# Value products always in split parts, a sixth head pair with float32 scores, and TensorE's products grouped by kind

## The chip, the cores and the metric

The kernel runs on one core of a Trainium2 chip. Its time is the device time of that core in microseconds (us); the median of three runs before the change is 1055.27 us (1054.64 to 1059.42). The core has a matrix engine (TensorE, PE in the rows, its weight loads PEld), a vector engine (VectorE, DVE), an engine for functions of one operand (ScalarE, ACT), a general one (GpSimd, POOL) and a queue that issues the DMAs (SyncE, SP). Each runs its own list of instructions in order and waits on semaphores for the others.

## The reference

Queries are averaged over pairs of rows, attention is taken in float32 for 4 batches of 8 heads (576 pooled queries, 1152 keys, 64 dimensions), and the result goes through two dense layers with a leaky ReLU between them.

```
q_pool = q.reshape(B, H, S // 2, 2, D).mean(axis=3)          # B 4, H 8, S 1152, D 64
scores = q_pool @ k.transpose(0, 1, 3, 2) / sqrt(D)
scores = scores - max(scores, axis=-1)
attn = exp(scores); attn = attn / (sum(attn, axis=-1) + 1e-9)
x = (attn @ v).transpose(0, 2, 1, 3).reshape(B * S // 2, H * D)   # 2304 x 512
h = x @ w_in                                                  # 512 x 2048
out = maximum(0.01 * h, h) @ w_out                            # 2048 x 512
```

## The kernel before

Results have to be as exact as float32. The kernel has two ways to a product. In the float32 way both operands stay float32. In the split way an operand is written as a first part, rounded to the shorter type fp32r, and a second part, the rest, and the products of the parts are summed in one bank of PSUM.

Attention is cut into 54 units, each one head with a group of its queries: a group of 256 rows (two tiles of 128) or one of 320 (tiles of 108, 106 and 106). For three batches the groups of 256 rows of all head pairs come first and those of 320 after. A segment is a head pair with one group (in the last batch with both); `PLAIN` is the number of segments, from the first one on, that work in float32. With `PLAIN = 5` these are units 0 to 7 (256 rows) and 8 and 9 (320 rows).

A unit runs through these steps. Queries are summed in pairs on GpSimd (`q_sum`, L370), transposed (`q_tr`, L378), and copied out of PSUM (`q_hi`, `q_lo`). Keys are transposed (`k_tr`, L328) and copied, whole for a float32 segment (`k_cp`) or in eight pieces of first and second parts (`k_hi`, `k_lo`, L343). `qk` makes the scores of a tile: in float32 two products of 512 columns and one of 128 (L428), in split parts six of 384 columns (L437 to L442). `vmax` takes the row maxima on VectorE (L453, and the last small one L457), `exp` the exponentials and their sums on ScalarE (L468). `tr` transposes the exponentials (L505); `e_hi` copies a transposed block to SBUF, in float32 on whichever of ScalarE and VectorE is free, in split parts as a cast on ScalarE, and `e_lo` then makes the second part on VectorE (L514). `pvm` multiplies by the values: in float32 one product a key tile (L525, two records each in the trace), in split parts two (L531) against a block that holds the first and second parts of the values side by side, 64 columns each. Those are made by `v_hi` (a cast on ScalarE or VectorE) and `v_lo` (L405, GpSimd). For a float32 segment `norm_plain` (L551, VectorE) multiplies by the reciprocal sums; for a split one `norm` first copies the lower half (ScalarE), adds it to the upper (L543, VectorE) and multiplies on GpSimd (L546).

Besides, 32 chunks of the weights are brought into shape and split (L579 to L604: ScalarE, VectorE twice, ScalarE, GpSimd, a cast, GpSimd), the first 16 for the first layer, which are stored in DRAM and read back, the others for the second. The two layers run over nine blocks of 256 rows: `l1` (L652) needs the block's rows of all heads, `l2` (L674 to L676) the split weights.

What stands where is decided by a planner written into the kernel, the class `Scheduler`. Each step has a rank (`prio`), costs on the engines that can do it, and the steps and buffers that it needs. The planner keeps a clock per engine, and of the steps that can start soonest takes the one of lowest rank. Ranks are counted in tiles of attention: `AHEAD` is how much earlier the preparation of a unit stands, `SOONER` the maxima and exponentials, `TR`, `SPLIT`, `PV` where transposes, splits and value products stand; `WIN` and `WOUT` place the weight chunks of the first and second layer (start and step), `WAHEAD` how many of them may be loaded ahead. `EARLY` is the unit from which the second score buffer is given to transposes and the layers. All that decides the order only; the waits come from what an instruction reads and writes.

Of the kernel before, what the change touches and what calls it, by code (L numbers as in the profile page):

```python
# [22 lines left out]
PLAIN = 5  # L23

KEEP = True
RT = 2.5
EARLY = 7
FIRST = 0
AHEAD = 4.0
# [3 lines left out]
WAHEAD = 3  # L33
WIN = (0.0, 1.0)
WOUT = (16.0, 0.6)
# [12 lines left out]
class Scheduler:  # L48
# [7 lines left out]
    def __init__(self, tags):  # L56
# [6 lines left out]
        self.done, self.log = set(), []  # L63

# [29 lines left out]
    def run(self):  # L94
# [4 lines left out]
        while left:  # L99
# [11 lines left out]
            s, e, at = min((x for x in can if x[2] <= now), key=lambda x: x[0].prio)  # L111
# [5 lines left out]
            left -= 1  # L117

    def start(self, s, e, at, pending):
# [11 lines left out]
        end = self.free[e] = at + s.eng[e]  # L131
# [25 lines left out]
def tile_pooled_attention_moe(  # L157
# [341 lines left out]

    def tr(u, x, e, i):  # L500
# [17 lines left out]
    def pvm(u, x, e, i=None):  # L518
# [197 lines left out]
    for u in range(NU):  # L716
# [8 lines left out]
        if u == us[0]:  # L725
# [68 lines left out]
        step(r_tr, u, prio=p0 + RT, eng=trs(*[64 for x in tiles_of(u)]), deps=[("rsum", u, 1)], takes=[("t", [("r_cp", u)])])  # L794
        step(r_cp, u, prio=p0 - 1, eng={"ACT": act(w, True)}, deps=[("r_tr", u)], takes=[("rb", [("norm_plain", u) if plain(u) else ("norm", u, 2)])])
        nx = len(kts(u))
        for x in range(nx):
            nk = len(kts(u)[x])
            step(tr, u, x, prio=p0 + TR, eng=trs(*[y[1] for y in tiles_of(u)] * nk),
                 deps=[("exp", u, t, x) for t in range(ntile) for x in range(2)], order=[("tr", u, x - 1)] if x else [("r_tr", u)] if RT < 0 else [], takes=[("t", [("e_hi" if plain(u) else "e_lo", u, x)])])  # L800
            step(e_hi, u, x, prio=p0 + SPLIT, eng={"ACT": act(w * nk, True), "DVE": dve(w * nk, psum=True)} if plain(u) else {"ACT": act(w * nk, True)}, deps=[("tr", u, x)], takes=[("et", [("pvm", u, x)])])
            if not plain(u):
# [96 lines left out]
```

## Time and profile before

| | |
|---|---|
| median of three runs | 1055.27 us |
| the profiled execution: its time, its span | 1055.03 us, 1053.2 us |
| mean granted TensorE clock | 0.988 |
| busy, TensorE | 998.6 us, 95% of the span |
| busy, VectorE / ScalarE / GpSimd | 701.8 / 642.0 / 382.8 us |
| chain that ended last: TensorE / VectorE / ScalarE | 81% / 10% / 3% |

A busy share over the whole span is an average over stages that have different bounds, so the rows further down cut it. In rows of TensorE the duration of an instruction is partly modelled; how long a group holds the engine is the time from its start to the start of the next.

### The profile page before, as it was taken

Reading aid. Unit: us, or ns where it says so; the run is one execution under the profiler, and the core shown is the slowest. Engines: PE = TensorE matmul, PEld = TensorE weight load, DVE = VectorE, ACT = ScalarE, POOL = GpSimd, SP = SyncE. Lnnn points to the kernel's source line nnn. Section 1 sums busy time; section 2 is a strip of 40 time slices with the busy share of each in tenths; the row PEclk is TensorE's granted clock in tenths of the full one; section 3 lists DMA queues with packets and bytes.
Section 4 is the critical chain, followed back from the end, with each engine's and each line's share of the span. In section 5 each row is a group of like instructions: output and inputs, shape, how many; then the busy total and the mean of one; then the engine's idle time right before and its main releaser. Section 6 shows DMA issues by size and latency. Waiting matters only on the chain.

```text
span 1053.2 us, 18894 instructions
## 1 busy us (share of the span) xinstructions
PE 998.6 (95%) x6676; PEld 870.8 (83%) x6676; DVE 701.8 (67%) x1479; ACT 642.0 (61%) x1558; POOL 382.8 (36%) x382
## 2 busy tenths in 40 slices
PE   6999788899999999999999999999999999999998
PEld 3555367789889988989899897989999998889896
DVE  4777889888888667777877676786877766411110
ACT  5767767776777665776767666776767666311110
POOL 3555666532434242223335233232342321232320
PEclk8999799999999999999999999999999999999999
DMA  8878673146376353635567253341533312477640
GB/s 266 288 237 261 231 243 128 51 167 228 111 263 225 100 185 107 233 97 173 174 209 245 77 177 101 123 163 38 182 99 98 110 56 86 147 239 250 213 148 30
DMA packets 86383, 172.68 MB, mean 164 GB/s; under 512 B 8976, under 2 KB 45328, under 8 KB 86288
## 3 DMA queue, kind: packets, MB, share of 16 engines
q1 hardware_dynamic: 86288, 171.47, 49.9%
q8 instruction: 52, 0.85, 0.3%
q14 instruction: 43, 0.35, 0.1%
HBM read 144.18 MB, written 27.26 MB: 163 GB/s over the span
## 4 chain that ended last, share of the span: by engine, by line
PE 81%; DVE 10%; ACT 3%; issue 3%; DMA 2%; POOL 1%; SPq 1%; DVEq 0%; ACTq 0%; POOLq 0%
PE banks L652 15%; PE banks L505 13%; PE banks L531 11%; PE banks L674 6%; PE banks L676 6%; PE banks L675 6%; PE banks L525 4%; PE banks L437 4%; PE banks L438 4%; DVE mx L453 3%; PE banks L428 3%; PE banks L441 2%; PE banks L442 2%; PE banks L328 2%; PE banks L486 2%
## 5 line engine op out<-in xcount | busy, mean ns | idle before, releaser
L453 DVE TENSOR_REDUCE mx<-banks 106x1 f32<-106x768 f32 (+4 forms) x320 | 235.3, 753 | 84.8 <-PE banks L438 45.7
L468 ACT ACTIVATE e<-banks,mx 106x768 f32<-106x768 f32 (+4 forms) x320 | 237.5, 744 | 54.2 <-DVE mx L457 47.4
L652 PE MATMUL banks<-xb,ws 128*128 128x256 f32 x1728 | 241.7, 285 | 11.3 <-ACT g L660 5.3
L652 PEld LDWEIGHTS banks<-xb,ws 128*128 128x128 f32 x1728 | 224.3, 190 | 19.7 <-ACT g L660 8.5
L200 ACT CAST et<-banks 128x320 fp32r<-128x320 f32 (+2 forms) x390 | 171.6, 466 | 101.2 <-PE banks L531 47.9
L514 DVE TENSOR_TENSOR et<-banks,et 128x320 fp32r<-128x320 f32 (+2 forms) x390 | 199.1, 528 | 50.5 <-ACT et L200 48.4
L505 PE MATMUL banks<-ident,e 128*128 128x128 f32 (+2 forms) x1440 | 204.6, 266 | 13.1 <-DVE mx L457 3.7
L531 PE MATMUL banks<-et,vv 128*128 128x320 f32 (+1 forms) x972 | 207.3, 320 | 3.2 <-DVE et L514 2.1
L505 PEld LDWEIGHTS banks<-ident,e 128*128 128x128 f32 (+2 forms) x1440 | 164.8, 141 | 50.8 <-DVE et L514 7.5
L531 PEld LDWEIGHTS banks<-et,vv 128*128 128x128 f32 x972 | 142.6, 189 | 6.9 <-DVE et L514 2.9
L370 POOL TENSOR_TENSOR qs<-qn 80x256 f32<-80x256 f32 (+1 forms) x128 | 75.6, 611 | 179.7 <-PE banks L378 100.3
L665 POOL TENSOR_TENSOR gg<-g,gg 128x512 fp32r<-128x512 f32 x60 | 77.8, 1297 | 155.9 <-DVE gg L200 112.7
L660 ACT ACTIVATE g<-banks 128x512 f32<-128x512 f32 x72 | 43.0, 597 | 99.9 <-PE banks L652 99.4
L405 POOL TENSOR_TENSOR vv<-vr,vv 128x576 fp32r<-128x576 f32 x46 | 66.3, 1442 | 100.0 <-DVE vv L200 65.9
L437 PE MATMUL banks<-kk,qq 128*106 128x384 f32 (+2 forms) x276 | 96.5, 350 | 2.0 <-ACT e L468 2.0
L674 PE MATMUL banks<-wo,gg 128*128 128x512 f32 x240 | 97.6, 407 | 0.0
L676 PE MATMUL banks<-wo,gg 128*128 128x512 f32 x240 | 94.4, 393 | 0.0
L675 PE MATMUL banks<-wo,gg 128*128 128x512 f32 x240 | 94.3, 393 | 0.0
L438 PE MATMUL banks<-kk,qq 128*106 128x384 f32 (+2 forms) x276 | 93.0, 337 | 0.0
L546 POOL TENSOR_TENSOR xo<-x,rb 64x320 f32<-64x320 f32 (+1 forms) x54 | 44.1, 816 | 71.6 <-DVE x L543 62.3
L468 ACT ACTIVATION_READ_ACCUMULATOR e<-banks,mx 128x1 f32 (+2 forms) x320 | 63.9, 200 | 0.0
L200 DVE CAST gg<-g 128x512 fp32r<-128x512 f32 x55 | 25.4, 462 | 47.8 <-ACT g L660 47.1
(70 smaller groups left out, 1364.1 us busy)
## 6 DMA issues: line engine op xcount, KB each, us to landing
ws<-wd SPq DMA_DIRECT2D x144, 512.0 KB, 4.5
vr<-in_v_dram SPq DMA_DIRECT2D x46, 288.0 KB, 3.4
kn<-in_k_dram SPq DMA_DIRECT2D x19, 576.0 KB, 4.1
kd<-kk SPq DMA_DIRECT2D x16, 576.0 KB, 5.2
kk<-kd SPq DMA_DIRECT2D x16, 576.0 KB, 4.1
raw<-in_moe_w_in_dram SPq DMA_DIRECT2D x16, 512.0 KB, 5.7
wd<-ws SPq DMA_DIRECT2D x16, 512.0 KB, 4.0
raw<-in_moe_w_out_dram SPq DMA_DIRECT2D x16, 512.0 KB, 6.3
```

The source lines that it names most:

```text
L200: ENG[e].copy(out=out, in_=in_) if e == "ACT" else ENG[e].tensor_copy(out=out, in_=in_)
L437: nc.tensor.matmul(p[:, c], lhsT=hi, rhs=key[:, c * CW:(c + 1) * CW], start=True, stop=False)
L438: nc.tensor.matmul(p[:, c], lhsT=lo, rhs=key[:, c * CW:(c + 1) * CW], start=False, stop=True)
L453: nc.vector.tensor_reduce(out=m[:, part:part + 1], in_=sps[u, j, part], axis=(AX.XY, AX.X)[part], op=ALU.max)
L468: nc.scalar.activation(out=d, in_=sps.pop((u, j, part)), func=AF.Exp, bias=mxs[u, j][:n, 2:3], accum_out=st[u][:n, c:c + 1])
L505: nc.tensor.transpose(p[:, a * w + o:a * w + o + n], ex[u, j][:n, t * 128:(t + 1) * 128], ident[:n, :n])
L514: nc.vector.tensor_tensor(out=et[u, x][:, 1, :w], in0=tps.pop((u, x))[:, :w], in1=f32(et[u, x])[:, 0, :w], op=ALU.subtract)
L531: nc.tensor.matmul(p, lhsT=vv[vis_of[u]][:, korder[vis_of[u] % 2][t], :], rhs=et[u, x][:, y, a * w:(a + 1) * w], start=(t == 0 and y == 0) ...
L652: nc.tensor.matmul(p, lhsT=wst[i, f][:, a, c, :], rhs=xx[i][:, x, c, :], start=(n == 0), stop=(n == 3 * KC - 1))
L674: nc.tensor.matmul(p, lhsT=gh, rhs=wo[f][:, 0], start=(f == hf * FH), stop=False)
L675: nc.tensor.matmul(p, lhsT=gh, rhs=wo[f][:, 1], start=False, stop=False)
L676: nc.tensor.matmul(p, lhsT=gl, rhs=wo[f][:, 0], start=False, stop=(f == hf * FH + FH - 1))
```

## The change

`PLAIN` becomes 6, so that the sixth segment (a head pair with its 320 rows: units 10 and 11, six tiles) also gets float32 scores. A second number, `PLAINV = 0`, decides about the values alone: no unit has float32 value products any more. So in units 0 to 9 every transposed block is cast on ScalarE and gets a second part on VectorE, the values go through `v_hi` and `v_lo`, and `norm` has its three steps. The planner marks the float32 score products as a kind of their own: a change of kind on TensorE costs `TURN` on its clock, and a step of the other kind stands `KIND` later in rank. Several numbers of ranks and costs move as well.

```
-PLAIN = 5
+PLAIN = 6
+PLAINV = 0
+TURN = 0.145
+KIND = 0.5
-EARLY = 7
+EARLY = 5
-AHEAD = 4.0
+AHEAD = 5.0
-WAHEAD = 3
+WAHEAD = 2
-WOUT = (16.0, 0.6)
+WOUT = (22.0, 0.8)
...
+        self.kinds, self.kind = set(), False
...
-            s, e, at = min((x for x in can if x[2] <= now), key=lambda x: x[0].prio)
+            s, e, at = min((x for x in can if x[2] <= now), key=self.urgency)
...
+    def urgency(self, x):
+        return x[0].prio + (KIND if x[1] == "PE" and (x[0].key in self.kinds) != self.kind else 0.0)
...
-        end = self.free[e] = at + s.eng[e]
+        end = at + s.eng[e]
+        if e == "PE" and (s.key in self.kinds) != self.kind:
+            self.kind = not self.kind
+            end += TURN
+        self.free[e] = end
...
+    def plain_v(hd):
+        return hd < 2 * PLAIN and hd % 4 < PLAINV
+
+    def plainv(u):
+        return plain_v(vis_of[u])
...
-        et[u, x] = new("et", i, F32 if plain(u) else None)
+        et[u, x] = new("et", i, F32 if plainv(u) else None)
...
-            if plain(u):
+            if plainv(u):
                 nc.tensor.matmul(
-                    p[0:64], lhsT=vv[vis_of[u]][:, (0, 2, 4, 6, 1, 3, 5, 7, 8)[t], :], rhs=et[u, x][:, 0, a * w:(a + 1) * w],
+                    p[0:64], lhsT=vv[vis_of[u]][:, key_tile(u, t), :], rhs=et[u, x][:, 0, a * w:(a + 1) * w],
...
-                eng = mm4(swidth(u)[part]) if plain(u) else mm(*[CW] * (2 if part else 4))
+                eng = {"PE": 0.3 if part else 1.045} if plain(u) else mm(*[CW] * (2 if part else 4))
...
+                if plain(u):
+                    sch.kinds.add(("qk", u, t, part))
...
-            if not plain(u):
+            if not plainv(u):
                 step(e_lo, u, x, prio=p0 + SPLIT, eng={"DVE": dve(w * nk, psum=True)}, deps=[("e_hi", u, x)])
...
-        if plain(u):
+        if plainv(u):
             step(norm_plain, u, prio=p0, eng={"DVE": dve(w, psum=True)}, deps=[("pvm", u, nx - 1), ("r_cp", u)], takes=[("xo", [("x_out", u)])])
```

What the planner makes of it is seen in the lists of instructions. First TensorE, late among the units of 256 rows, before (banks are PSUM; e are the exponentials, et their transposed blocks, vv the values, kk and qq keys and queries, kn keys as loaded, stat the reciprocals of the sums):

```order
L428 MATMUL banks<-kk,qq 128x128
L328 MATMUL banks<-ident,kn 128x128 x3
L525 MATMUL banks<-et,vv 64x256 x2
L328 MATMUL banks<-ident,kn 128x128 x3
L486 MATMUL banks<-ident,stat_67 64x128 x2
L525 MATMUL banks<-et,vv 64x256 x3
L378 MATMUL banks<-ident,qs 128x80 x4
L428 MATMUL banks<-kk,qq 128x512 x2
L505 MATMUL banks<-ident,e 128x128 x4
```

and TensorE at about the same place after:

```order
L527 MATMUL banks<-ident,e 128x128 x4
L447 MATMUL banks<-kk,qq 128x128
L527 MATMUL banks<-ident,e 128x128 x10
L553 MATMUL banks<-et,vv 128x256 x8
L447 MATMUL banks<-kk,qq 128x512 x2
L505 MATMUL banks<-ident,stat_66 64x128 x2
L553 MATMUL banks<-et,vv 128x256 x4
L447 MATMUL banks<-kk,qq 128x128
L347 MATMUL banks<-ident,kn 128x128 x3
```

Of the nine rows before, four are of the float32 kind (L428, L525) and change with transposes at nearly every row; after, only the three rows of scores (L447) are, and the value products (L553, now two a key tile and 128 columns of values) stand with the transposes. Over the whole list changes of kind fall from 126 to 88. Next VectorE among the same units, before (mx are maxima, raw and ws weights, et the transposed blocks; the number behind a name is the buffer's):

```order
L457 TENSOR_REDUCE mx_681<-mx_681 128x1
L453 TENSOR_REDUCE mx_711<-banks_63 128x1
L200 CAST ws_723<-raw_643 128x512
L588 SCALAR_TENSOR_TENSOR raw_699<-raw_522,raw_699 128x512
L200 COPY et_732<-banks_63 128x512
L200 COPY et_738<-banks_63 128x256
L453 TENSOR_REDUCE mx_711<-banks_63 128x1
L457 TENSOR_REDUCE mx_711<-mx_711 128x1
```

and VectorE there after:

```order
L476 TENSOR_REDUCE mx_561<-mx_561 128x1
L610 SCALAR_TENSOR_TENSOR raw_599<-raw_457,raw_599 128x512
L536 TENSOR_TENSOR et_607<-banks_63,et_607 128x512
L536 TENSOR_TENSOR et_615<-banks_63,et_615 128x512
L472 TENSOR_REDUCE mx_633<-banks_63 128x1
L213 CAST ws_643<-raw_599 128x512
L606 TENSOR_SCALAR raw_647<-raw_589 128x512
L610 SCALAR_TENSOR_TENSOR raw_647<-raw_496,raw_647 128x512
L536 TENSOR_TENSOR et_656<-banks_63,et_656 128x256
L472 TENSOR_REDUCE mx_633<-banks_63 128x1
L496 SCALAR_TENSOR_TENSOR stat1_66<-stat1_66 128x2
```

Some plain copies of blocks (L200 COPY et) are gone from VectorE; in their place every block has its second part there (L536). Last GpSimd at the place where the first queries of 320 rows are summed (qs), before:

```order
L370 TENSOR_TENSOR qs<-qn 80x4x64 x2
L604 TENSOR_TENSOR ws<-raw,ws 128x512
L595 TENSOR_TENSOR raw<-raw 128x512
L604 TENSOR_TENSOR ws<-raw,ws 128x512
L595 TENSOR_TENSOR raw<-raw 128x512
L370 TENSOR_TENSOR qs<-qn 80x4x64 x2
```

and after:

```order
L568 TENSOR_TENSOR xo<-x_818,rb 64x256
L424 TENSOR_TENSOR vv<-vr,vv 128x9x64
L626 TENSOR_TENSOR ws<-raw,ws 128x512
L389 TENSOR_TENSOR qs<-qn 80x4x64 x2
L617 TENSOR_TENSOR raw<-raw 128x512
L626 TENSOR_TENSOR ws<-raw,ws 128x512
L389 TENSOR_TENSOR qs<-qn 80x4x64 x2
```

Between the same weight steps there now stand second parts of values (L424) and products with the reciprocals (L568).

## Rows read from the trace of the kernel before

**Rows 1.** Busy time by stage: length, PE, PEld, DVE, ACT, POOL (instructions), PEclk, DMA share, GB/s

```profile
0.00:97.00 97.00, 86.86 (x422) 47.96 (x423) 63.02 (x130) 63.87 (x142) 47.74 (x58) 0.96 0.83 267
97.00:195.00 98.00, 83.55 (x466) 57.58 (x464) 86.34 (x154) 69.42 (x161) 66.96 (x54) 0.91 0.54 184
195.00:247.50 52.50, 50.03 (x368) 46.40 (x368) 42.12 (x93) 37.86 (x99) 16.55 (x19) 1.00 0.47 155
247.50:900.00 652.50, 631.88 (x4496) 587.70 (x4495) 488.04 (x1057) 447.17 (x1114) 212.58 (x226) 1.00 0.45 144
```

**Rows 2.** The same view of line 457 alone (DVE), one row maximum a tile

```profile
0.00:97.00 97.00, 2.41 (x16) 0.96 0.83 267
97.00:195.00 98.00, 2.24 (x15) 0.91 0.54 184
195.00:247.50 52.50, 1.30 (x9) 1.00 0.47 155
```

**Rows 3.** Timeline, DVE's first row: start, length, engine, line, operation, count, idle before

```profile
9.03 1.42 DVE L453 TENSOR_REDUCE mx<-banks 128x1 f32<-128x1024 f32 x2 [9.03 <-PE banks L428]
```

**Rows 4.** Chain that ended last, from 97 to 195 us, shares by line

```profile
by line: PE banks L525 16.5%; DVE mx L453 10.6%; issue 10.0%; PE banks L505 9.6%; PE banks L428 8.6%; DVE raw L584 6.4%; DVE wo L200 4.7%; POOL raw L595 3.6%; DVE kk L343 3.4%; ACT e L468 3.0%; DVE raw L588 2.8%; DVE stat L477 2.3%; DVE et
```

**Rows 5.** Timeline of PE among the units of 256 rows

```profile
88.36 1.13 PE L428 MATMUL banks<-kk,qq 64*128 64x512 f32 x4
89.42 0.66 PE L505 MATMUL banks<-ident,e 128*128 128x128 f32 x4
90.01 0.49 PE L428 MATMUL banks<-kk,qq 64*128 64x128 f32 x2
90.43 0.66 PE L505 MATMUL banks<-ident,e 128*128 128x128 f32 x4
...
93.09 1.94 PE L525 MATMUL banks<-et,vv 128*64 128x256 f32 x8
94.97 0.44 PE L505 MATMUL banks<-ident,e 128*128 128x128 f32 x2
...
101.87 1.08 PE L525 MATMUL banks<-et,vv 128*64 128x256 f32 x4
102.88 0.44 PE L505 MATMUL banks<-ident,e 128*128 128x128 f32 x2
```

**Rows 6.** Timeline of PE in a later unit of 256 rows, in split parts

```profile
271.05 0.60 PE L505 MATMUL banks<-ident,e 128*128 128x128 f32 x4
271.41 0.73 PE L531 MATMUL banks<-et,vv 128*128 128x256 f32 x4
271.97 0.38 PE L505 MATMUL banks<-ident,e 128*128 128x128 f32 x2
...
272.67 0.34 PE L437 MATMUL banks<-kk,qq 128*128 128x384 f32 x1
...
273.71 0.38 PE L486 MATMUL banks<-ident,stat 128*64 128x128 f32 x2
```

**Rows 7.** Groups of DVE by shape: line, operation, count, busy us, mean ns, idle before

```profile
L514 DVE TENSOR_TENSOR et<-banks,et 128x320 fp32r<-128x320 f32 x270 | 126.0, 483 | 40.3 <-ACT et L200 38.4
L514 DVE TENSOR_TENSOR et<-banks,et 128x512 fp32r<-128x512 f32 x96 | 63.7, 680 | 6.9 <-ACT et L200 6.6
L200 DVE CAST vv<-vr 128x576 fp32r<-128x576 f32 x33 | 24.8, 751 | 20.1 <-PE banks L531 17.1 <-POOL qs L370 1.4 <-issue 1.3
```

**Rows 8.** Groups of DVE, shapes together: the plain copies of blocks

```profile
L200 DVE COPY et<-banks 128x512 f32<-128x512 f32 (+2 forms) x25 | 14.1, 565 | 6.8 <-PE banks L505 4.0 <-PE banks L525 1.3 <-ACT raw L579 1.1
```

**Rows 9.** The page's costliest groups: ACT's casts of blocks, POOL's second parts of values

```profile
L200 ACT CAST et<-banks 128x320 fp32r<-128x320 f32 (+2 forms) x390 | 171.6, 466 | 101.2 <-PE banks L531 47.9
L405 POOL TENSOR_TENSOR vv<-vr,vv 128x576 fp32r<-128x576 f32 x46 | 66.3, 1442 | 100.0 <-DVE vv L200 65.9
```

**Rows 10.** One weight step on DVE, 0 to 97 us, then 97 to 195 us

```profile
L584 DVE TENSOR_SCALAR raw<-raw 128x512 uint32<-128x512 uint32 x15 | 7.9, 532 | 2.3 <-ACT raw L579 2.3
...
L584 DVE TENSOR_SCALAR raw<-raw 128x512 uint32<-128x512 uint32 x17 | 15.1, 892 | 0.0
```

More of the change, by code (lines that the diff above doesn't have):

```diff
@@ L498, in kts, with key_tile @@
         return [(0, 1), (2, 3), (4, 5), (6, 7), (8,)] if units[u][2] == 0 else [(t,) for t in range(KT)]
+    def key_tile(u, t):
+        return (0, 2, 4, 6, 1, 3, 5, 7, 8)[t] if plain(u) else korder[vis_of[u] % 2][t]
     def tr(u, x, e, i):
@@ L531, in pvm @@
                 nc.tensor.matmul(
-                    p, lhsT=vv[vis_of[u]][:, korder[vis_of[u] % 2][t], :], rhs=et[u, x][:, y, a * w:(a + 1) * w],
+                    p, lhsT=vv[vis_of[u]][:, key_tile(u, t), :], rhs=et[u, x][:, y, a * w:(a + 1) * w],
                     start=(t == 0 and y == 0), stop=(t == KT - 1 and y == 1),
@@ L692, in mm @@
     def mm(*cols):
-        return {"PE": sum(0.0035 + 0.000445 * max(c, 240) for c in cols)}
+        return {"PE": sum(0.0045 + 0.000445 * max(c, 240) for c in cols)}
     def mm4(*cols):
-        return {"PE": sum(0.01 + 0.00182 * c for c in cols)}
+        return {"PE": sum(0.01 + 0.00169 * c for c in cols)}
     def trs(*rows):
-        return {"PE": sum(0.01 + 0.00077 * r for r in rows)}
+        return {"PE": sum(0.006 + 0.000805 * r for r in rows)}
     def act(n, psum=False):
@@ L793, in tile_pooled_attention_moe @@
         step(rsum, u, 1, prio=p0, eng={"DVE": 0.17}, deps=[("rsum", u, 0)])
-        step(r_tr, u, prio=p0 + RT, eng=trs(*[64 for x in tiles_of(u)]), deps=[("rsum", u, 1)], takes=[("t", [("r_cp", u)])])
-        step(r_cp, u, prio=p0 - 1, eng={"ACT": act(w, True)}, deps=[("r_tr", u)], takes=[("rb", [("norm_plain", u) if plain(u) else ("norm", u, 2)])])
+        step(r_tr, u, prio=p0 + RT, eng=trs(*[x[1] for x in tiles_of(u)]), deps=[("rsum", u, 1)], takes=[("t", [("r_cp", u)])])
+        step(r_cp, u, prio=p0 - 1, eng={"ACT": act(w, True)}, deps=[("r_tr", u)], takes=[("rb", [("norm_plain", u) if plainv(u) else ("norm", u, 2)])])
         nx = len(kts(u))
@@ L799, in tile_pooled_attention_moe @@
             step(tr, u, x, prio=p0 + TR, eng=trs(*[y[1] for y in tiles_of(u)] * nk),
[L800 to L802 removed]
+                 deps=[("exp", u, t, x) for t in range(ntile) for x in range(2)], order=[("tr", u, x - 1)] if x else [("r_tr", u)] if RT < 0 else [], takes=[("t", [("e_hi" if plainv(u) else "e_lo", u, x)])])
+            step(e_hi, u, x, prio=p0 + SPLIT, eng={"ACT": act(w * nk, True), "DVE": dve(w * nk, psum=True)} if plainv(u) else {"ACT": act(w * nk, True)}, deps=[("tr", u, x)], takes=[("et", [("pvm", u, x)])])
+            if not plainv(u):
                 step(e_lo, u, x, prio=p0 + SPLIT, eng={"DVE": dve(w * nk, psum=True)}, deps=[("e_hi", u, x)])
             before = ("pvm", u, x - 1) if x else ("pvm", prev, len(kts(prev)) - 1) if u else None
[L805 to L808 removed]
+            done = [("e_hi", u, x), ("load_vv", hd)] if plainv(u) else [("e_lo", u, x), ("v_lo", hd)]
+            if plainv(u):
+                sch.kinds.add(("pvm", u, x))
+            step(pvm, u, x, prio=p0 + PV, eng=mm4(*[w] * nk) if plainv(u) else mm(*[w] * (2 * nk)), deps=done + [before],
+                 takes=[("o", [("norm_plain", u) if plainv(u) else ("norm", u, 1)])] if x == 0 else [])
+        if plainv(u):
             step(norm_plain, u, prio=p0, eng={"DVE": dve(w, psum=True)}, deps=[("pvm", u, nx - 1), ("r_cp", u)], takes=[("xo", [("x_out", u)])])
```

13 lines of the change are left out of this document (6 added, 7 removed).

## The prediction

> **What bounds the kernel now.** I read first the busy time by stage, with the stages cut by the row maxima, so that each is the same work before and after [rows 1, 2]. A "tile" is one block of up to 128 query rows of one head; its scores end in one small reduction on VectorE, and these are counted: 16 up to 97 us (stage A: the eight units of 256 rows, all in float32, while the weights of the first layer are split), 15 more up to 195 us (stage B: the first five units of 320 rows, where float32 gives way to split parts, and the second layer's weights), 9 more up to 247.5 us (stage C). The remaining 805 us (stage D) do the rest of attention and nearly all of the two layers. The reader is to see that the bound changes hands. In A TensorE is busy 86.9 of 97 us; VectorE, whose first work starts at 9.0 us [rows 3], only 63. In B it is the other way: VectorE 86.3 of 98 us, TensorE 83.6, and that at a mean granted clock of 0.91. In C and D TensorE is busy 95 to 97% at full clock, VectorE 75 to 80%.
>
> Next, the chain through B [rows 4]: TensorE's float32 value products are 16.5% of it, but VectorE's maxima, weight steps and key parts together weigh more than any TensorE line. In B two masters alternate.
>
> Last, TensorE's own rows in A and in D, read start to start since its ends are modelled [rows 5, 6]. In A eight records of the float32 value product (two records make one product) hold 1.88 us, four hold 1.01: 0.435 us a product and 0.14 us once per group, for going back from float32 to transposes. Four transposes ahead of a float32 group take 0.59 us; four ahead of a split group take 0.36. So going into float32 costs 0.23 us, and a change of kind 0.185 us on the mean of both directions. A split product (two records) of 256 columns takes 0.28 us (0.56 for four records).
>
> **The change part by part.** Counts of instructions are from the two orders, durations from rows.
>
> TensorE. 72 float32 value products of 256 columns become split ones: 72 x (0.435 - 0.28) = 11.2 us less. 18 of 320 columns, scaled by 1.25: 3.5 us less. Changes of kind fall from 126 to 88: 38 x 0.185 = 7.0 us less. The sixth head pair's six tiles get float32 scores: 1.06 + 0.42 less two leavings of 0.14 is 1.20 us, against six split products in 1.04 us (272.67 to 273.71): 1.0 us more. Sum: 20.7 us less, of which 16.8 in A (58 products before, 54 after, 36 fewer changes of kind).
>
> VectorE. Every transposed block of the first ten units now needs a second part [rows 7]: 32 of 512 columns at 0.680, 18 of 320 at 0.483 and 8 of 256 at under that, 34 us more. The 25 plain copies that it did go to ScalarE as casts: 14.1 us less [rows 8]. Seven of the ten new first parts of the values: 7 x 0.751 = 5.3 us more [rows 7]. The sixth pair no longer needs second parts of keys (eight pieces, about the sizes of a 256- to 320-wide second part, so near 3.6 us) and of queries (two, near 1.0). Sum: about 20 us more. By stage, counted in the orders up to the same tile: A 31 second parts, 14 copies fewer, 7 casts, one weight chunk fewer: 15 us by these means, of which back-to-back overlap leaves some 14. B: 22 more second parts of 320, nine more of the other widths, 11 copies fewer, but three weight chunks fewer (14, not 17): 5 us more. C: level.
>
> ScalarE gets the 25 casts, 25 x 0.466 = 11.7 us [rows 9], and ten copies of the lower half of the sum, some 4 us. It was busy 63.9 of 97 and 69.4 of 98 us [rows 1]: hidden. GpSimd gets ten second parts of values, 10 x 1.442 = 14.4 us [rows 9], and ten products with the reciprocals that VectorE did, each under one such part; some 17 us of it lie in A and early B, where GpSimd had 49 and 31 us free [rows 1]. Hidden as work, not as a neighbour (below). SP issues the same number of DMAs; values now land in their own buffer and not in the operand's. The wait this adds: the first value product of a unit now waits for a cast and a GpSimd subtraction. Queued behind it on TensorE are transposes and scores, but the values are loaded a unit ahead, so I cost it at 0; with that cover gone it is at most 0.75 + 1.44 us a unit, some 18 us for eight units.
>
> Now the stages.
> A: TensorE's 86.9 us shrink to 70, so it stops being the bound. VectorE has 63.0 + 14 = 77 us to do from the moment the first scores exist (9.0 us). At 100% that ends at 86 us; at the share it held in B when it was the bound (86.3 of 98, 88%) at 96.5. I take 93%, between the two, since in B it also waited for a slow TensorE: 9 + 77/0.93 = 92. A: 5 us less (bounds 9 less, 8 more, the latter explained below).
> B: 86.3 + 5 = 91.3 us of VectorE work in 98 us; the float32 value products on the chain get shorter, and the stretch at half clock should shrink. I take 0 (bounds 6 less, 6 more: at the old idle time VectorE would need 103).
> C: TensorE-bound; the order puts about 4 us less TensorE work between the same two tiles (fewer value products and transposes). I take 3 us less (0 to 4).
> D: the orders have the same number of layer products left at tile 40 to within 11 records, so TensorE's work left is equal. 0, with 4 either side for the shifted order.
> Sum: 8 us less. The profiled execution took 1055.03 us (span 1053.2), 0.24 below the median of the runs, so its own time serves: 1055 - 8 = 1047 us. TensorE loses 21 us of work and the kernel 8, since VectorE inherits the bound.
>
> A row that speaks against the change: one and the same weight step on VectorE took 0.532 us in A and 0.892 in B [rows 10], where GpSimd's busy share was 49% and 68% [rows 1]. After, GpSimd's share in A comes near 65%. If A's 14 weight chunks and its casts took B's longer durations, the steps alone would add 14 x 0.36 = 5 us, and the casts and second weight step about as much again: 10 to 13 us, the upper bound of A.
> The Trainium skill has a rule for it, "SBUF — State Buffer", section "Who interferes with whom": copies, casts and tensor-scalar steps of VectorE in their two-port mode take the port pair that GpSimd uses, and whichever comes second is blocked outright until the other ends. The trace agrees in kind (the mean grows with GpSimd's share). By that rule the new casts and GpSimd parts raise the price on both sides, which is the third rival.
>
> **The rivals.**
> 1. The whole TensorE gain comes out: 1055 - 21 = 1034. For it: TensorE is the largest share of every stage but B. Against it: by tile 40 VectorE would have 191.5 + 20 = 211 us of work [rows 1] in 247.5 - 21 - 9 = 217.5 us, 97% busy; it reached 88% when it was the bound.
> 2. No change, 1056: VectorE's 20 us take back exactly what TensorE gives. That holds if VectorE stays at 88% in A and B: A ends at 96.5, B takes 5 us more, C 3 less, 1.5 more in all. For it: that share is the one on record. Against it: in B part of the idle time was TensorE at half clock.
> 3. Slower, 1065. Place: VectorE's weight steps and casts in A, blocked by GpSimd. Price: about 10 us in A, so that VectorE needs 9 + 87/0.93 = 102.5 us (5.5 more), plus 6 in B, less 3 in C, plus the value wait not quite covered (2): about 10 more. It decides from the point where VectorE's work in A passes 82 us (9 + 82/0.93 = 97).
> That the change does not do what it says is not open: the orders show the float32 value products gone and the groups longer.
>
> **How the numbers follow.** About 0.5% (5.3 us) is what a measurement of this kernel can tell from no change: faster is below 1050.0, slower above 1060.5. My forecast, 1042 to 1050, 0.42; the whole gain, below 1042, 0.13; no change 0.27; slower 0.18. So faster 0.55, same 0.27, slower 0.18. The range of 1035 to 1064 reaches from the whole gain to the slower rival and leaves out some 0.15; the forecast's own range is 1042 to 1050.
>
> **What would show it.** Right: the sixteenth tile's maximum near 92 us with VectorE over 85% busy and TensorE near 75% in that stage; the 31st near 190; the 40th near 239; TensorE's busy total some 20 us down and VectorE's some 20 up; the stretch from tile 40 to the end unchanged at 805 us. Rival 1: tile 40 before 230 us. Rival 3: the weight steps' means in A above 0.8 us. I am wrong in the mechanism if TensorE waits in A for anything but VectorE's results (ScalarE's casts, or the values' second part on GpSimd), if the granted clock falls in A after 25 us, or if stage D moves by more than 4 us.

## The result: slower, where I forecast faster

The changed kernel took 1065.32 us (median of 4 runs, 1064.55 to 1070.94) against 1054.95 us (4 runs) before: ratio 1.0102, 95% interval 1.0057 to 1.0147. I said 1047 us and faster. The third rival's place (VectorE's weight steps in stage A) and its 1065 us are what came, and I had given it 0.18; its terms did not come one by one (see the last point of the account below).

The profiled execution has a span of 1062.8 us, 9.6 more than before. The page gives the engines' busy time:

```profile
PE 989.4 (93%) x6676; PEld 879.1 (83%) x6676; DVE 739.4 (70%) x1513; ACT 653.4 (61%) x1587; POOL 408.7 (38%) x402
```

TensorE fell from 998.6 to 989.4 us, not by 20.7; VectorE rose by 37.6 us, not by 20. By stage, cut at the same row maxima (16th, 31st, 40th, 160th), so that each row answers to one of [rows 1]:

```profile
0.00:105.20 105.20, 77.67 (x401) 52.31 (x401) 89.83 (x152) 68.57 (x155) 63.91 (x69) 0.85 0.72 237
105.20:207.10 101.90, 84.93 (x517) 65.24 (x518) 91.08 (x168) 76.14 (x179) 67.09 (x56) 0.90 0.55 187
207.10:259.50 52.40, 47.09 (x328) 43.51 (x326) 43.68 (x90) 38.09 (x94) 28.18 (x27) 0.93 0.51 167
259.50:904.90 645.40, 628.19 (x4481) 583.13 (x4480) 492.13 (x1059) 446.99 (x1116) 209.76 (x223) 1.00 0.45 144
```

The columns are length, PE, PEld, DVE, ACT, POOL, granted clock, DMA share, GB/s. The kernel before, cut at its own 16th, 31st and 40th maximum:

```profile
0.00:96.40 96.40, 86.26 (x419) 47.57 (x420) 62.86 (x129) 63.27 (x141) 47.53 (x57) 0.96 0.83 266
96.40:194.30 97.90, 83.61 (x463) 57.43 (x461) 86.02 (x153) 69.32 (x160) 66.48 (x53) 0.91 0.54 187
194.30:247.10 52.80, 50.16 (x368) 46.54 (x369) 42.19 (x94) 38.24 (x100) 16.85 (x19) 1.00 0.46 155
```

From there to its end are 806.1 us. So A is 8.8 us longer, B 4.0, C 0.4 shorter, and the rest (645.4 + 157.9 = 803.3) 2.8 shorter: 9.6 in all. So the loss lies in A and B. In A VectorE is busy 89.8 of 105.2 us and only 62.9 of 96.4 before, while the granted clock fell from 0.96 to 0.85.

Which of VectorE's work grew in A? Its groups by shape up to the 16th maximum (count, busy, mean ns of one), of the changed kernel:

```profile
L536 DVE TENSOR_TENSOR et<-banks,et 128x512 fp32r<-128x512 f32 x25 | 16.6, 679 | 1.4 <-ACT et L213 1.3
L610 DVE SCALAR_TENSOR_TENSOR raw<-raw 128x512 uint32<-128x512 uint32 x14 | 14.6, 1052 | 0.1
L606 DVE TENSOR_SCALAR raw<-raw 128x512 uint32<-128x512 uint32 x14 | 13.1, 940 | 0.8 <-ACT raw L601 0.8
L213 DVE CAST ws<-raw 128x512 fp32r<-128x512 f32 x12 | 7.5, 628 | 0.0
L496 DVE SCALAR_TENSOR_TENSOR stat<-stat 128x2 f32<-128x2 f32 x7 | 6.1, 874 | 0.0
L213 DVE CAST vv<-vr 128x576 fp32r<-128x576 f32 x7 | 5.2, 741 | 0.1
```

and of the kernel before, the rows that are not in [rows 10]:

```profile
L588 DVE SCALAR_TENSOR_TENSOR raw<-raw 128x512 uint32<-128x512 uint32 x15 | 10.2, 688 | 0.2
L200 DVE CAST ws<-raw 128x512 fp32r<-128x512 f32 x12 | 5.0, 417 | 0.0
L477 DVE SCALAR_TENSOR_TENSOR stat<-stat 128x2 f32<-128x2 f32 x7 | 3.7, 535 | 0.8 <-ACT e L468 0.8
```

The new work (second parts, casts of values) has the durations of [rows 7]. What grew is work that the change doesn't touch: the two weight steps, the weight casts and the sums of a row's exponentials, 41.3 us in place of 26.8, and that for one chunk fewer. One and the same trace shows what they grew beside. Of the changed kernel's 28 weight steps in A, six have no GpSimd instruction beside them: one L606 at 0.43 us and five L610 at 0.68 on the mean, the prices of before (0.42 and 0.69 where nothing was beside them). The other 13 and 9 take 0.98 and 1.26 us on the mean.

The timeline shows how one such step grew (start, length, engine, line):

```profile
66.23 0.86 POOL L568 TENSOR_TENSOR xo<-x,rb 64x256 f32<-64x256 f32 x1 [2.67 <-DVE x L565]
...
66.40 3.54 DVE L606 TENSOR_SCALAR raw<-raw 128x512 uint32<-128x512 uint32 x1
...
67.05 1.39 POOL L424 TENSOR_TENSOR vv<-vr,vv 128x576 fp32r<-128x576 f32 x1
...
68.41 1.25 POOL L626 TENSOR_TENSOR ws<-raw,ws 128x512 fp32r<-128x512 f32 x1
...
69.87 0.27 DVE L472 TENSOR_REDUCE mx<-banks 128x1 f32<-128x128 f32 x1
...
70.67 0.13 DVE L476 TENSOR_REDUCE mx<-mx 128x1 f32<-128x2 f32 x1
...
70.80 1.11 PE L527 MATMUL banks<-ident,e 128*128 128x128 f32 x4 [2.36 <-DVE mx L476]
```

L606's fastest take 0.40 us. This one ends only when three GpSimd instructions, back to back, have ended (68.41 + 1.25 = 69.66 us): the product with the reciprocals and the values' second part, both new here, and a weight half. The row maximum stands behind it (L472 and, after one second part, L476), and TensorE waits 2.36 us until L476. TensorE pays in its clock as well:

```profile
60.00:65.00 5.00, 3.18 (x17) 1.82 (x17) 4.97 (x10) 3.55 (x10) 2.65 (x2) 1.00 0.51 150
65.00:70.00 5.00, 3.02 (x12) 1.97 (x12) 5.00 (x6) 2.12 (x6) 3.44 (x3) 0.58 0.67 204
70.00:75.00 5.00, 4.20 (x14) 2.48 (x15) 2.88 (x7) 2.26 (x4) 2.12 (x3) 0.50 0.85 263
```

The granted clock fell from full speed, 2.4 GHz, to 0.50 of it, 1.2 GHz, at 65.8 us and rose at 76.0. So the 3.54 us step, which began at 66.40, did not bring it down. Before the fall TensorE was busy 3.65 of the 5 us up to 60 and 3.18 of the 5 up to 65, with two longer waits for VectorE:

```profile
58.13 0.44 PE L527 MATMUL banks<-ident,e 128*128 128x128 f32 x2 [1.06 <-DVE et L536]
...
65.42 0.82 PE L527 MATMUL banks<-ident,e 128*128 128x128 f32 x4 [1.84 <-DVE kk L213]
```

The wait for the long step then falls into the slow stretch, and two float32 score products take 2.08 us instead of the 1.13 in [rows 5]:

```profile
71.56 1.20 PE L553 MATMUL banks<-et,vv 128*128 128x256 f32 x4
72.69 2.08 PE L447 MATMUL banks<-kk,qq 64*128 64x512 f32 x4
```

There are four such stretches in A after 25 us, of 6.8, 10.2, 3.4 and 3.4 us (the last begins at 96.5); before, there is none there. The runs below tie them to the split values in A: all four others that have these (e2, e3, e4, e7) have such stretches there, and none of the eight with float32 values has.

The Trainium skill, "SBUF — State Buffer", section "Who interferes with whom", has a second rule beside the one in the prediction: a VectorE instruction with two inputs in SBUF contends with a GpSimd instruction that reads SBUF. The trace agrees: L610 and L496 are such instructions, and their means rose from 0.688 to 1.052 and from 0.535 to 0.874 us; all eight L610 in A that took over 0.69 us have a GpSimd instruction beside them.

### The profile page after: what moved, and what is told of

It reads as the page before. It is cut to its first block, busy times and chain, and to the rows that moved or that the text cites. A ratio compares the mean times of both kernels' runs of the same rounds, so it can differ in the third digit from the quotient of the medians.

```text
span 1062.8 us, 19001 instructions
## 1 busy us (share of the span) xinstructions
PE 989.4 (93%) x6676; PEld 879.1 (83%) x6676; DVE 739.4 (70%) x1513; ACT 653.4 (61%) x1587; POOL 408.7 (38%) x402
## 4 chain that ended last, share of the span: by engine, by line
PE 75%; DVE 14%; ACT 3%; issue 3%; DMA 2%; POOL 1%; SPq 1%; DVEq 0%; POOLq 0%; ACTq 0%
PE banks L674 16%; PE banks L553 13%; PE banks L527 12%; PE banks L696 6%; PE banks L698 6%; PE banks L697 6%; PE banks L456 4%; DVE mx L472 4%; PE banks L457 4%; PE banks L447 2%; PE banks L460 2%; DVE et L536 2%; PE banks L461 2%; PE banks L505 1%; ACT e L487 1%
## 5 line engine op out<-in xcount | busy, mean ns | idle before, releaser
L472 DVE TENSOR_REDUCE mx<-banks 106x1 f32<-106x768 f32 (+4 forms) x320 | 234.5, 752 | 65.3 <-PE banks L457 38.3
L536 DVE TENSOR_TENSOR et<-banks,et 128x320 fp32r<-128x320 f32 (+2 forms) x448 | 232.7, 536 | 62.4 <-ACT et L213 59.9
L213 ACT CAST et<-banks 128x320 fp32r<-128x320 f32 (+2 forms) x448 | 199.4, 470 | 112.1 <-PE banks L553 53.9
L553 PE MATMUL banks<-et,vv 128*128 128x320 f32 (+1 forms) x1152 | 247.1, 324 | 2.8 <-DVE et L536 1.9
L527 PE MATMUL banks<-ident,e 128*128 128x128 f32 (+2 forms) x1440 | 210.8, 271 | 33.3 <-DVE et L536 12.9
L553 PEld LDWEIGHTS banks<-et,vv 128*128 128x128 f32 x1152 | 171.3, 194 | 10.4 <-DVE et L536 3.7
L424 POOL TENSOR_TENSOR vv<-vr,vv 128x576 fp32r<-128x576 f32 x56 | 80.6, 1440 | 149.8 <-DVE vv L213 95.5
L456 PE MATMUL banks<-kk,qq 128*106 128x384 f32 (+2 forms) x264 | 94.8, 359 | 5.8 <-ACT e L487 5.6
L696 PE MATMUL banks<-wo,gg 128*128 128x512 f32 x236 | 95.9, 406 | 1.0 <-ACT g L682 0.9
L698 PE MATMUL banks<-wo,gg 128*128 128x512 f32 x236 | 92.9, 394 | 0.0
L697 PE MATMUL banks<-wo,gg 128*128 128x512 f32 x236 | 92.8, 393 | 0.0
L457 PE MATMUL banks<-kk,qq 128*106 128x384 f32 (+2 forms) x264 | 89.4, 339 | 0.0
L213 DVE CAST gg<-g 128x512 fp32r<-128x512 f32 x56 | 31.1, 556 | 56.2 <-ACT g L682 55.7
L568 POOL TENSOR_TENSOR xo<-x,rb 64x256 f32<-64x256 f32 (+1 forms) x64 | 52.3, 817 | 40.6 <-DVE x L565 22.3
L487 ACT ACTIVATION_READ_ACCUMULATOR e<-banks,mx 128x1 f32 (+2 forms) x320 | 63.9, 200 | 0.0
```

The source lines that it names most:

```text
L213: ENG[e].copy(out=out, in_=in_) if e == "ACT" else ENG[e].tensor_copy(out=out, in_=in_)
L456: nc.tensor.matmul(p[:, c], lhsT=hi, rhs=key[:, c * CW:(c + 1) * CW], start=True, stop=False)
L457: nc.tensor.matmul(p[:, c], lhsT=lo, rhs=key[:, c * CW:(c + 1) * CW], start=False, stop=True)
L472: nc.vector.tensor_reduce(out=m[:, part:part + 1], in_=sps[u, j, part], axis=(AX.XY, AX.X)[part], op=ALU.max)
L487: nc.scalar.activation(out=d, in_=sps.pop((u, j, part)), func=AF.Exp, bias=mxs[u, j][:n, 2:3], accum_out=st[u][:n, c:c + 1])
L536: nc.vector.tensor_tensor(out=et[u, x][:, 1, :w], in0=tps.pop((u, x))[:, :w], in1=f32(et[u, x])[:, 0, :w], op=ALU.subtract)
```

## The experiments

Theory 1: the second parts and casts move more work to VectorE in A, where GpSimd's new work also blocks VectorE's weight steps; float32 values are better there. Rivals: VectorE's own load alone, the new ranks, the sixth pair, or the grouping. All kernels by stage (A, B, C and the rest in us of the profiled execution; median of the runs; ratio to the runs of before on the same chip):

| kernel | float32 values in units | score pairs | A | B | C | rest | median | ratio, 95% |
|---|---|---|---|---|---|---|---|---|
| before | 10 | 5 | 96.4 | 97.9 | 52.8 | 806.1 | 1054.95 | |
| changed | 0 | 6 | 105.2 | 101.9 | 52.4 | 803.3 | 1065.32 | 1.0102 |
| e1 | 12 | 6 | 94.8 | 108.3 | 47.5 | 810.4 | 1063.20 | 1.0108 [1.0090, 1.0126] |
| e2 | 0 | 5 | 108.6 | 90.0 | 51.0 | 811.6 | 1060.81 | 1.0080 [1.0056, 1.0104] |
| e3, old ranks | 0 | 6 | 100.2 | 120.7 | 53.0 | 809.9 | 1086.27 | 1.0328 [1.0306, 1.0350] |
| e4, short sign step | 0 | 6 | 104.0 | 98.4 | 52.4 | 801.6 | 1059.19 | 1.0068 [1.0052, 1.0085] |
| e5 | 10 | 5 | 98.8 | 104.0 | 50.1 | 813.4 | 1063.14 | 1.0077 [1.0054, 1.0101] |
| e6 | 8 | 6 | 95.2 | 94.7 | 45.6 | 806.9 | 1043.81 | 0.9892 [0.9857, 0.9928] |
| e7, no new GpSimd work | 0 | 6 | 95.5 | 97.7 | 55.9 | 810.0 | 1057.99 | 1.0039 [1.0013, 1.0065] |
| e8, before + GpSimd work | 10 | 5 | 96.3 | 103.8 | 56.1 | 806.4 | 1061.94 | 1.0083 [1.0060, 1.0107] |
| e9 | 8 | 5 | 97.6 | 94.4 | 52.4 | 805.8 | 1049.34 | 0.9963 [0.9946, 0.9980] |
| e10 | 10 | 6 | 94.8 | 101.4 | 46.4 | 807.3 | 1051.61 | 0.9977 [0.9957, 0.9996] |
| e11, no grouping | 8 | 6 | 98.3 | 96.3 | 51.2 | 811.5 | 1059.26 | 1.0059 [1.0039, 1.0078] |
| e12 | 8 | 7 | 94.8 | 102.2 | 48.3 | 812.6 | 1058.96 | 1.0053 [1.0026, 1.0080] |

The stages are those of one execution, which in e2, e5, e7, e8 and e9 took 2.1 to 4.9 us longer than the median. The kernel before had a median of 1052.50 us beside e1 to e4, 1053.98 beside e5 to e8 and 1054.07 beside e9 to e12, so between these sets the ratio is the safer comparison.

**e1, float32 values back in all twelve units of the six pairs.**

```diff
-PLAINV = 0
+PLAINV = 4
```

> The changed kernel with float32 value products in units 0 to 11 again (PLAINV = 4); the sixth pair's float32 scores, the new ranks and the grouping by kind stay. Theory (the split values load VectorE and GpSimd in the first 97 us): the sixteenth tile's maximum falls from 105 to 97 us or sooner, VectorE's busy share up to it from 85% to 70% or less, and the kernel takes 1050 to 1056 us. Rival (the new order of the list costs it): it stays at 1062 us or more, with the sixteenth maximum still past 102 us.

A is back at 94.8 us, as the theory said, with VectorE at 74.4 (78%, where 70% or less was asked): the loss of A comes from the split values. But the total is 1063.20, 7 us over the theory's range and in the rival's, since B grew to 108.3 us; TensorE is its master there, busy 97.0:

```profile
0.00:94.80 94.80, 85.75 (x431) 49.75 (x432) 74.42 (x139) 65.22 (x145) 56.15 (x64) 0.96 0.87 293
94.80:203.10 108.30, 97.01 (x493) 58.72 (x491) 81.52 (x146) 64.77 (x151) 58.87 (x49) 0.91 0.48 156
```

**e2, five pairs of float32 scores.**

```diff
-PLAIN = 6
+PLAIN = 5
```

> The changed kernel with split scores for the sixth pair again (PLAIN = 5); the values stay in split parts everywhere, with the new ranks and the grouping. Theory (the values are the cause): within 3 us of the changed kernel (1062 to 1068), the sixteenth maximum at 105 us as there. Rival (the float32 scores of the sixth pair cost it): back to 1056 us or less, with stage B (maxima 17 to 31) shorter by 5 us or more.

4.5 us faster than the changed kernel by the medians, but the two intervals overlap (1.0056 to 1.0104 and 1.0057 to 1.0147); still slower than before. The total lies between theory and rival. B is the shortest of all (90.0 us), as the rival said, A the longest (108.6): the sixth pair isn't what A loses by.

**e3, the old ranks.**

```diff
-EARLY = 5
+EARLY = 7
-AHEAD = 5.0
+AHEAD = 4.0
-WAHEAD = 2
+WAHEAD = 3
-WOUT = (22.0, 0.8)
+WOUT = (16.0, 0.6)
```

> The changed kernel with the four rank numbers of before (EARLY 7, AHEAD 4, WAHEAD 3, WOUT 16 and 0.6); split values, six pairs and the grouping stay. Theory (values): 1060 to 1070 us, the sixteenth maximum past 102 us. Rival (the moved ranks cost it): 1057 us or less.

Both totals are missed: the new ranks are worth 21 us beside split values. With the old ones, which bring the second layer's weights sooner, VectorE did 18 first and 19 second weight steps in B instead of 14 each and was busy 103.7 of 120.7 us there:

```profile
100.20:220.90 120.70, 94.94 (x530) 71.88 (x530) 103.72 (x176) 81.11 (x185) 83.24 (x67) 0.86 0.52 181
```

**e4, GpSimd's sign step on 64 of 512 columns.**

```diff
-nc.gpsimd.tensor_tensor(out=wt[i], in0=wt[i], in1=wy[i], op=ALU.mult)
+nc.gpsimd.tensor_tensor(out=wt[i][:, 0:64], in0=wt[i][:, 0:64], in1=wy[i][:, 0:64], op=ALU.mult)
```

> The changed kernel, but GpSimd's sign step on the weights works on 64 of the 512 columns (the sign is left out of the others), so that 32 steps of 1.29 us shrink to some 0.4 us; VectorE has the same instructions. Theory (VectorE is blocked by GpSimd in stage A): the means of its two weight steps up to the sixteenth maximum fall from 0.94 and 1.05 us to under 0.75 and 0.85, the sixteenth maximum comes 5 us or more sooner (100 us or less), and the kernel takes 1058 us or less. Rival (VectorE's own added work, blocking or not): the sixteenth maximum within 2 us of 105 and the kernel within 3 us of 1065.

GpSimd's busy time in A fell from 63.9 to 50.2 us, yet the two weight steps kept their means, a miss; casts and sums fell:

```profile
0.00:104.00 104.00, 75.55 (x401) 50.39 (x401) 86.55 (x153) 68.24 (x155) 50.19 (x69) 0.93 0.74 240
L610 DVE SCALAR_TENSOR_TENSOR raw<-raw 128x512 uint32<-128x512 uint32 x14 | 14.6, 1050 | 0.1
L606 DVE TENSOR_SCALAR raw<-raw 128x512 uint32<-128x512 uint32 x14 | 13.5, 969 | 0.6 <-ACT raw L601 0.6
L213 DVE CAST ws<-raw 128x512 fp32r<-128x512 f32 x12 | 5.7, 475 | 0.0
L496 DVE SCALAR_TENSOR_TENSOR stat<-stat 128x2 f32<-128x2 f32 x7 | 4.3, 615 | 0.0
```

So GpSimd's busy share does not set the price; what stands beside each step does. Only three of the changed kernel's 28 weight steps in A had the sign step (L617), which is what this edit shortens, beside them. The 3.5 us step stood there as before, beside L568, L424 and L626. A is 1.2 us shorter, as the rival said, and the kernel 6.1 us faster, between the two; these intervals overlap too. That led to e7.

**e5, the new order with the old products.**

```diff
-PLAIN = 6
+PLAIN = 5
-PLAINV = 0
+PLAINV = 4
```

> The changed order alone: the new ranks, the grouping of products by kind and the new prices in the planner, but float32 scores for five head pairs and float32 values in their ten units, as before. Theory 1 (the loss comes from the products: VectorE's split parts beside more GpSimd work in stage A, and sixth-pair work in stage B): with the old products the new order costs nothing, so 1050 to 1056 us, 16th maximum at 93 to 97 us, 31st at 188 to 195. Rival (the new ranks themselves lose, for instance by weights that come at a worse time or a tail that starts later): 1059 us or more, with the loss between the 31st maximum and the end.

Here the rival holds in the total: 9 us slower with the products of before. Its place is half right: in the profiled execution, itself 4.9 us over the median, A loses 2.4, B 6.1, the rest 7.3 us, and C gains 2.7. The new order is no gain by itself; e3 says that the old ranks are far worse with the new products.

**e6, float32 values in the eight units of stage A only.**

```diff
-return hd < 2 * PLAIN and hd % 4 < PLAINV
+return hd < 8
```

> The changed kernel, but the eight units of 256 rows (stage A) keep float32 values; the units of 320 rows, four of which have float32 values before, have split ones. Theory 1 (A loses by VectorE and GpSimd, B loses by float32 values at 320 rows when the sixth pair's scores come on top): A as in the run with float32 values in all twelve units (16th maximum at 95 us), B as in the changed kernel or a little shorter (98 to 102 us, against 108 in that run), so 1054 to 1059 us. Rival (what A gains is lost again later, since the weights and the layers' work set the end): A at 95 but 1061 us or more.

Faster than both kernels, and than either theory said. The 31st maximum comes at 189.9 us, the 40th at 235.5:

```profile
0.00:95.20 95.20, 85.11 (x431) 49.31 (x432) 73.13 (x139) 65.34 (x145) 56.28 (x64) 0.96 0.88 294
95.20:189.90 94.70, 82.60 (x474) 60.12 (x472) 85.41 (x162) 68.15 (x161) 64.30 (x50) 0.91 0.51 175
189.90:235.50 45.60, 44.66 (x330) 41.96 (x328) 35.39 (x82) 33.25 (x87) 17.20 (x19) 1.00 0.44 147
```

The changed kernel has TensorE 7.4 us less busy in A, VectorE 16.7 us more, and is 10.0 us later, although this one does more weight steps there (18 and 17 against 14 and 14). At the 40th tile it is 24.0 us behind this one, at the 160th 19.4: the whole difference arises in A to C. C belongs to it, since the changed kernel still has four weight chunks to do there and this one has one, and VectorE is busy 43.7 against 35.4 us. What A's slow weight steps don't finish is paid later.

**e7, the changed kernel without its new GpSimd work.**

```diff
+if e == "ACT":                                 # in v_lo, for the first ten heads
+    copy(e, vv[hd][:, :, D:2 * D], vn.pop(hd))
...
-step(norm, u, 2, prio=p0, eng={"POOL": gp(w)}, ...
+step(norm, u, 2, prio=p0, eng={"DVE": dve(w)} if hd < 10 else {"POOL": gp(w)}, ...
```

> The changed kernel without its new GpSimd work among the first ten units: the values' second part is a cast on ScalarE (0.67 us each; it writes the cast values in the place of the remainder), the product with the reciprocals is on VectorE (ten more of about 0.4 us). Theory 1 (GpSimd's ten second parts of values and ten products stand back to back with its weight halves and block VectorE's weight steps): the steps' means in A fall from 0.94 and 1.05 us to at most 0.7 and 0.8, the longest from 3.5 us to under 2; although VectorE gets 4 us more work, A ends 4 to 8 us earlier (97 to 101 us), total 1056 to 1061. Rival (VectorE has too much work of its own in A, whoever its neighbour is): means above 0.85 us, A at 104 us or later, total 1065 or more.

Theory 1 holds, in the means and in the total; A ends 1.5 us sooner than it said:

```profile
L613 DVE SCALAR_TENSOR_TENSOR raw<-raw 128x512 uint32<-128x512 uint32 x13 | 9.4, 728 | 0.0
L609 DVE TENSOR_SCALAR raw<-raw 128x512 uint32<-128x512 uint32 x13 | 8.7, 672 | 0.2 <-POOL raw L620 0.2
```

```profile
0.00:95.50 95.50, 75.26 (x405) 50.44 (x405) 77.01 (x151) 70.76 (x159) 42.70 (x53) 0.91 0.74 239
95.50:193.20 97.70, 80.21 (x468) 59.41 (x466) 86.49 (x167) 73.10 (x173) 54.68 (x46) 0.88 0.61 206
193.20:249.10 55.90, 51.04 (x354) 45.79 (x354) 49.12 (x101) 40.79 (x100) 33.73 (x29) 1.00 0.48 150
```

VectorE has the same second parts and casts in A, and a few products more, but is busy 77.0 us instead of 89.8, and A ends 9.7 us sooner. Some of that is a chunk and four weight casts fewer, which at these means are some 3 us of the 12.8. The longest L609 up to the 16th maximum is 1.53 us instead of 3.54. The kernel still isn't ahead of before: it has done 26 of the first weight steps by the 31st maximum (28 in the changed kernel, 32 before), and C and the rest give 10 us back. The planner lays out the order anew for this kernel, so a part of these shifts is the order's. The prices alone don't hang on that: here too the steps with nothing of GpSimd beside them take 0.42 and 0.69 us, and there are 15 of them instead of six.

**e8, the kernel before with GpSimd's new work added.**

```diff
+nc.gpsimd.tensor_tensor(out=d, in0=vv[hd], in1=vv[hd], op=ALU.subtract)
+nc.gpsimd.tensor_tensor(out=new("t1", i)[:, :width(u)], in0=xos[u], in1=xos[u], op=ALU.mult)
```

> The kernel before, with the same amount of GpSimd work added among the first ten units that the change adds there: ten subtractions of 576 columns and ten products of 256 to 320 columns, their results not used, and nothing added on VectorE, ScalarE or TensorE. Theory 1 (GpSimd's neighbours set the price of VectorE's weight steps): means in A rise from 0.53 and 0.69 us to 0.8 or more; VectorE has room in A, so the total rises by 0 to 4 us (1053 to 1057). Rival (the steps are slow after the change because VectorE's own split parts crowd them): means stay under 0.65 and 0.8, total within 1 us of before.

The means rise, with nothing added on VectorE; the first nearly to the 0.8 that was asked, the second above it:

```profile
L591 DVE TENSOR_SCALAR raw<-raw 128x512 uint32<-128x512 uint32 x15 | 11.6, 779 | 0.1
L595 DVE SCALAR_TENSOR_TENSOR raw<-raw 128x512 uint32<-128x512 uint32 x14 | 11.5, 828 | 0.1
```

A doesn't move (96.3 us), since TensorE is the bound there and VectorE had room. The total is a miss, 5 us over the range: B is 5.9 us longer and C 3.3. How much of that is GpSimd's and how much the order, which the planner lays out anew around the added steps, this run doesn't tell. The edit also lets each unit's store wait for the added product, and its block of values stay until the added subtraction.

**e9, e6 with five pairs.**

```diff
-PLAIN = 6
+PLAIN = 5
```

> The fastest version so far (1043.8 us: the new order, float32 scores for six pairs, float32 values in the first eight units alone), with float32 scores for five pairs. Theory 1 (the gain lies in split values for the ninth and tenth unit, where VectorE and a slow TensorE alternated; the sixth pair's scores are worth little): A the same (95 us), B 94 to 98 us, total 1043 to 1049 us. Rival (the sixth pair is what makes stage B and C short, by freeing VectorE of second parts of keys and queries): tile 40 at 241 us or later, total 1052 or more.

Between the two: the sixth pair is worth 5.5 us, in A and C (97.6 and 52.4 against 95.2 and 45.6), and with five pairs split values in units nine and ten 13.8 (e5 against e9). What the sixth pair is worth hangs on the values: 11.5 us with float32 values in ten units (e5 against e10), 5.5 with eight, and no gain with none (e2).

**e10, e6 with float32 values in ten units.**

```diff
-return hd < 8
+return hd < 10
```

> The fastest version so far with float32 values in ten units, the set of the kernel before, and float32 scores for six pairs: so this is the change without any change to the values. Theory 1 (split values in the ninth and tenth unit make the gain): A 95 us, B 101 us or more (104 with five pairs, 108 with all twelve units in float32 values), total 1054 to 1063 us. Rival (the sixth pair makes it): B under 98 us, total under 1050.

Theory 1 holds in B and misses the total by 2 us. The ninth and tenth unit in split values are worth 7.8 us (1051.61 less 1043.81), 6.7 of them in B:

```profile
94.80:196.20 101.40, 88.66 (x492) 59.86 (x491) 86.92 (x149) 69.58 (x162) 62.18 (x48) 0.93 0.49 166
```

Against e6's second row TensorE is busy 6.1 us more and VectorE 1.5 more. So in B the split values take from TensorE without adding to VectorE's total.

**e11, e6 without grouping by kind.**

```diff
-TURN = 0.145
-KIND = 0.5
+TURN = 0.0
+KIND = 0.0
```

> The fastest version so far without the grouping of TensorE's products by kind (no penalty for a change of kind, no price for it). Theory 1 (a change of kind costs 0.185 us and the grouping saves some 20 to 40 of them): 3 to 8 us slower in A and B, 1047 to 1052 us. Rival (grouping is worth nothing here, since TensorE is not alone the bound in A and B, or since it delays what VectorE waits for): 1043 us or less.

15 us slower, more than either said. Changes of kind in A, counted in the order, are 81 against 63; 18 x 0.185 = 3.3 us, and A is 3.1 us longer. B has fewer changes than e6 (33 against 41) and is still 1.6 us longer; C is 5.6 longer and the rest 4.6. So the price of a change of kind fits A alone, where VectorE also did fewer weight steps (16 and 16 against 18 and 17); the other 12 us come with the other order, by a way that no run here isolates.

**e12, e6 with seven pairs.**

```diff
-PLAIN = 6
+PLAIN = 7
```

> The fastest version so far with float32 scores for seven pairs. Theory 1 (scores in float32 cost TensorE 0.17 us a tile more than split ones and free VectorE of about 4.6 us of second parts a pair; from tile 25 or so on VectorE is not the bound alone): within 3 us of 1043.8 (1041 to 1047). Rival (float32 scores run beside VectorE's idle time and only lengthen TensorE, as stage B with all twelve units in float32 values did): 1048 us or more.

The rival holds: B is 102.2 us, TensorE busy 89.4 of it.

```profile
94.80:197.00 102.20, 89.40 (x505) 64.76 (x504) 88.12 (x158) 70.00 (x165) 65.83 (x54) 0.88 0.48 163
```

## Why the prediction was wrong, point by point

- **What bounds the kernel: right.** A by TensorE, B by both in turns. With split values VectorE takes over A (89.8 of 105.2 us).
- **VectorE's new work in A, 14 us: right, but it is not all that A got.** The step that failed is "VectorE has 63.0 + 14 = 77 us to do". It priced VectorE's unchanged steps as they were before. The rows that grew add 41.3 - 26.8 = 14.5 us, and 77 + 14.5 = 91.5 is near the 89.8 measured. In e7, with GpSimd's new neighbours gone, it is 77.0 (with one chunk fewer). Of the 17.6 us between forecast and measured, A has 13.8, B 4.0 and C 2.6, and the rest takes 2.8 off.
- **"I take 93%": right.** From 9 us to 105.2 VectorE was busy 93% (89.8 of 96.2); 9 + 91.5/0.93 = 107. The share was good and the load was wrong. The share is luck in part: a step that waits for GpSimd counts as busy, so the share holds the very wait that I left out. I had the row that said so [rows 10], worked out 10 to 13 us from it, and left it at the edge of the range.
- **GpSimd "hidden as work, not as a neighbour": the right sentence, the wrong consequence.** I looked at free time on GpSimd. The cost depends on which VectorE step stands beside GpSimd's work, above all an unbroken run of it (the prices with and without a neighbour in one trace; e4, e7, e8).
- **TensorE 16.8 us less in A: 8.6 measured** (86.3 to 77.7). Two items were right in kind: changes of kind fell from 85 to 49 in A, and a split product is cheaper. But TensorE waited for VectorE, the granted clock fell to 0.50 in four stretches after 25 us, 23.9 us in all, and score products in them took up to twice as long (2.08 us for 1.13). TensorE was busy 20.3 us in these stretches; at that ratio 9 us of them are the clock's (an estimate), which is about the 8 that are missing. I had named that fall as a sign that I am wrong in the mechanism. TensorE did wait mainly for VectorE, as I said (14.9 us of its idle time in A, 1.0 before), though also 5.3 us for ScalarE's exponentials (3.6 before).
- **B level: wrong, 4.0 us longer.** VectorE's load rose by 5.1 us, as I had it, and its share went from 88 to 89%. I set the 5 against a stretch at half clock that should shrink; the clock went from 0.91 to 0.90. Split values in B are not what costs: e6 has them there too, in units 8 to 11, and a B of 94.7 us. In e7, without the new GpSimd work, B is 97.7, as long as before, which points to GpSimd here too; since its C is 3.1 us longer than before, that is not shown.
- **C 3 us less: 0.4.** Four weight chunks slid into it from A and B.
- **Rest unchanged: 2.8 us less,** inside the 4 either side.
- **The wait for the values' second part, at 0: right.** No value product waits for it in A or B; one load for query transposes does, for 0.9 us. As a neighbour of VectorE's steps the second part does count.
- **Rival 3:** its sum was 5.5 + 6 - 3 + 2; measured 8.8 + 4.0 - 0.4 and 2.8 less in the rest, with no value wait. The place and its mechanism were right; that the sum meets the 1065 us is luck. Its point of decision (82 us of VectorE work in A) was passed by 8 us.

What the change does is then a sum of parts that I had treated as one. With six pairs and the new order, 0, 8, 10 and 12 units with float32 values give 1065.3, 1043.8, 1051.6 and 1063.2 us. The first eight units in split values cost 21.5 us; the other two of before gain 7.8. Open are the other 12 us of the grouping, what makes B longer in the changed kernel, and why the stretch after tile 40 moves between 801.6 and 813.4 us with orders that leave it nearly the same work. The clock is at most a part of that: in e1, e5 and e11 (810.4 to 813.4 us) it stood at 0.50 for 6.8 us there, but in e2 and e12 (811.6 and 812.6) for 3.4.

## What to carry to other kernels

Before moving work to an engine with free time, ask what its instructions will stand beside: price the neighbours' existing steps at the durations they have where both engines are busy, not only the added ones. Where a product can be done in two ways, choose by the stage's bound: here split values cost 21.5 us in the eight units of stage A, where they take VectorE from 73 to 90 us of work, and gain 7.8 in the two units after, where they leave it about level (86.9 to 85.4). Where one row of the profile already shows the higher price, put it into the sum.

## What the runs showed of the hardware

- One VectorE step can wait out a whole run of GpSimd instructions, not just the one that it meets: 3.54 us beside 0.86 + 1.39 + 1.25 = 3.50 us back to back, against 0.40 us at its fastest. It does not always: an L606 of 0.78 us from 55.01 us on ended at 55.79, after the first of two (53.84 to 55.51, 55.47 to 56.92).
- Small instructions aren't spared. A sum on 128 x 2 elements (0.145 us with nothing of GpSimd beside it) took 2.71 us, up to the end of two GpSimd instructions at 94.14 us:

```profile
91.44 2.71 DVE L496 SCALAR_TENSOR_TENSOR stat<-stat 128x2 f32<-128x2 f32 x1
```
